# Softmax sums of eight heads per visit to the column-tiled array, in an attention block with program-ordered transfers and a warmed TensorE

## The chip, the cores and the metric

One Trainium2 chip, one core of it. The metric is the device time of one execution in microseconds (us), lower is better. The engines are called PE (TensorE, the matmuls), PEld (its weight loads), DVE (VectorE), ACT (ScalarE), POOL (GpSimd) and SP (SyncE, whose queue issues most transfers).

## The reference

A transformer block with adaptive layer norm: 2048 tokens, width 1024, 32 query heads on 4 key/value heads of 128, the last 512 cached positions, and a SwiGLU feed-forward part (FFN) of width 3584.

```python
mod = (silu(c) @ w_mod).reshape(1, 6, 1, -1)
sa, ca, ga, sb, cb, gb = mod[:, 0], ..., mod[:, 5]
h = layernorm(x) * (1 + ca) + sa
q = h @ wq                                    # 32 heads of 128
p = softmax(q @ k.T * 128 ** -0.5)            # last 512 of 2048 cached positions
x = x + ga * ((p @ v) @ wo)
h = layernorm(x) * (1 + cb) + sb
x = x + gb * ((silu(h @ w_gate) * (h @ w_up)) @ w_down)
```

The inputs and the output are bf16.

## The kernel before

The tokens go in four chunks of 512 (`NTC` = 4), and the attention is a loop over `NU` = 128 steps, one for each head `g` of each chunk. A step computes scores and their exponentials, the projection q of a head three steps ahead, and the output o of the head before. Beside that it does "tasks" that a plan has put at that step. No maximum is subtracted: a bound on the scores (`bound_wq`, `bound_k`, `bound_final`) is computed on the side, and a general path runs if it fails (it does not here).

The softmax denominator of a head is a sum over 512 positions. DVE adds four tiles to one (`psB`), and a matmul with 32 columns of ones sums over the partitions. Four heads make one "visit": their four matmuls sit side by side in a column-tiled array. ACT inverts the sums as exp(-ln), a transfer writes them to DRAM, another reads them back broadcast to all partitions (`rb`, two heads in each), and DVE multiplies the outputs `oT`.

```python
    def emit_l(g):                       # every fourth head
        l_ps = mm("l_ps")
        for i in range(4):
            nc.tensor.matmul(l_ps[32 * i:32 * i + 32, :], lhsT=ones_bf[:, 0:32],
                             rhs=rec.pop(g - 3 + i), start=True, stop=True)
        r = wk.tile([P, TCW], FP32, name="rinv", tag="f32", bufs=2)
        nc.scalar.activation(out=r, in_=l_ps, func=ACT.Ln)
        nc.scalar.activation(out=r, in_=r, func=ACT.Exp, scale=-1.0)
        d = dp.tile([4, TCW], FP32, name="r_d", tag="r_d", bufs=4)
        nc.scalar.dma_start(out=d, in_=r[0:P:32, :])
        rinv[g // 4] = d

    def load_rb(g):                      # two heads later
        ...
        for i in range(2):
            rb = wk.tile([P, 2, TCW], FP32, name="rb", tag="rb", bufs=2)
            nc.sync.dma_start(out=rb, in_=d[2 * i:2 * i + 2, :].partition_broadcast(P))
            rinv[g // 4].append(rb)

    def emit_norm(g):                    # four heads later
        o = oT[(g // H, (g % H) // 4)]
        for i, rb in enumerate(rinv.pop(g // 4)):
            oo = o[:, 2 * i:2 * i + 2, :]
            nc.vector.tensor_tensor(out=oo, in0=oo, in1=rb, op=ALU.mult)
# ... (cut)
    for g in range(3, NU, 4):
        at(g + 2, load_rb, g)
        at(g + 4, emit_norm, g)
    for cc in range(NTC):
        for q in range(NQ):                        # output projection, groups of HQ = 8 heads
            s0 = cc * H + q * HQ + HQ + 4
            for dh in range(DH):
                at(s0 + 4 * dh - 4, load_wo, cc, q, dh)
            for u in range(2 * QT):
                at(s0 + u, emit_wo, cc, q, u)      # one a_ps tile: eight matmuls on oT of 8 heads
        plan_ln((cc + 1) * H + 12, ("h2", cc), cb1, sb)
# ... (cut)
    for k in range(NU + 1):
        if k % 4 == 2 and k + 6 < NU:
            load_wq((k + 6) // H, ((k + 6) % H) // 4)
        if k < NU:
            emit_s(k)
        if k + LEAD < NU:
            emit_q(k + LEAD)
        ...
        run_tasks(k)
        if k >= 1:
            if k % 4 == 0:
                emit_l(k - 1)
            emit_o(k - 1)
```

At the start the first 512 tokens are normalised tile by tile, transposed on PE, and the modulation vectors are made with 128x1 matmuls; then 24 q matmuls of the first three heads run before the loop.

```python
    for t in range(QT):
        ln_stats(t)
        n = ln_norm(t, t % 2 == 0)
        for dt in range(DT):
            nc.tensor.transpose(h0_ps[dt // 4][:, dt % 4, t * P:(t + 1) * P],
                                n[:, dt * P:(dt + 1) * P], ident)
    # ... (cut: modulation columns, then)
        for n in range(4 * LEAD):
            dt, g = (4 * half + n // LEAD, n % LEAD) if half == 0 else (4 + n % 4, n // 4)
            nc.tensor.matmul(q0_ps[g], ...)
```

The kernel leaves the order of instructions on the engines and in the queue of transfers to a scheduler.

Of the kernel before, what the change touches and what calls it, by code (L numbers as in the profile page):

```python
# [9 lines left out]
ALU = mybir.AluOpType  # L10
# [578 lines left out]
def fast_path(ctx, tc, flag, A_x, A_k_cache, A_v_cache, A_wq, A_wo, B_x, B_w_gate, B_w_up,  # L589
# [65 lines left out]
    def load(out, in_, eng=None):  # L655
        with nc.allow_non_contiguous_dma(reason="weight slice"):
            (eng or nc.sync).dma_start(out=out, in_=in_)
# [8 lines left out]
    def load_x(tt):  # L666
        nc.sync.dma_start(out=xt[tt], in_=x2d[tt * P:(tt + 1) * P, :])
# [23 lines left out]
    for kv in range(Hkv):  # L691
        nc.sync.dma_start_transpose(out=kT[:, kv, :], in_=A_k_cache[0, kv, k0:k0 + W, :])
# [11 lines left out]
    nc.vector.memset(eps_t, eps)  # L704
    modT = const.tile([P, 4, DT], FP32, name="modT")
    sa, ca1, sb, cb1 = (modT[:, i, :] for i in range(4))
    ga_bc = const.tile([P, D], FP32, name="ga_bc")
    gb_bc = const.tile([P, D], FP32, name="gb_bc")
# [35 lines left out]
    def load_rows(vecs, part):  # L744
        wm_rows.append([])
        for vec in vecs:
            t = hpool.tile([P, 4, D], BF16, name="wmr", tag="hT")
            load(t, wm_v[:, 4 * part:4 * part + 4, vec * D:(vec + 1) * D])
            wm_rows[-1].append(t)

    def mod_rows(n, part):
        ps = mm("row_ps")
        tiles = wm_rows.pop()
# [9 lines left out]
        else:  # L763
# [3 lines left out]
            nc.sync.dma_start(out=d, in_=r[0:P:32, :])  # L767
            row_d[n] = d

    def load_gate(n, k, dst):  # L770
        nc.sync.dma_start(out=dst.rearrange("p (a b) -> p a b", a=2),
                          in_=row_d[n][k:k + 2, :].partition_broadcast(P))

    def load_cols(n, k, dst, add_one):
        src = row_d[n][k:k + 2, :].rearrange("a (b p) -> p (a b)", p=P)
        with nc.allow_non_contiguous_dma(reason="1024 values to columns"):
            nc.sync.dma_start(out=dst, in_=src)
# [12 lines left out]
    def ln_stats(tt):  # L790
        st = sm.tile([P, DH, nc.vector.BN_STATS_DIM], FP32, name="st", tag="st")
        for i in range(DH):
            nc.vector.bn_stats(out=st[:, i, :], in_=xt[tt][:, i * 512:(i + 1) * 512])  # L793
# [6 lines left out]
    def ln_norm(tt, on_act=False):  # L800
# [7 lines left out]
        else:  # L808
            nc.vector.tensor_scalar(out=n, in0=xt[tt], scalar1=mv[:, 0:1], scalar2=mv[:, 2:3],
                                    op0=ALU.subtract, op1=ALU.mult)  # L810
# [7 lines left out]
    def ln_xpose(key, tt):  # L818
        t = tt % QT
        if t == 0:  # L820
            new_hT(key)
        nc.sync.dma_start_transpose(out=hT[key][:, :, t * P:(t + 1) * P], in_=xn.pop(tt))

    def ln_affine(key, dt, ps, sc, sh, on_act):
# [3 lines left out]
        else:  # L828
            nc.vector.tensor_scalar(out=hT[key][:, dt, :], in0=ps, scalar1=sc[:, dt:dt + 1],
                                    scalar2=sh[:, dt:dt + 1], op0=ALU.mult, op1=ALU.add)  # L830
# [4 lines left out]
    def new_hT(key):  # L835
        hT[key] = hpool.tile([P, DT, TCW], BF16, name="hT", tag="hT")

# [24 lines left out]
# [3 lines that stand above are left out]
        for dt in range(DT):  # L865
            nc.tensor.transpose(h0_ps[dt // 4][:, dt % 4, t * P:(t + 1) * P],
                                n[:, dt * P:(dt + 1) * P], ident)
    q0_ps = []
# [20 lines left out]
    def bound_wq(hg, i, j):  # L889
        w = wq_tiles[(0, hg, i)][:, 2 * j:2 * j + 2, :]  # L890
        junk = wk.tile([P, 2, 512], BF16, name="junk", tag="psA", bufs=2)
        col = (hg * 2 + i) * 2 + j
        nc.vector.scalar_tensor_tensor(out=junk, in0=w, scalar=1.0, in1=w, op0=ALU.mult,  # L893
                                       op1=ALU.mult, accum_out=sq[:, col:col + 1])
# [6 lines left out]
    def bound_k():  # L901
        kk = sm.tile([P, Hkv * WT], FP32, name="kk", tag="kk", bufs=1)
        for i in range(Hkv * WT):
            junk = wk.tile([P, Dh], BF16, name="junk", tag="psA", bufs=2)
            src = k_ld[0][:, i // WT, i % WT, :]
            nc.vector.scalar_tensor_tensor(out=junk, in0=src, scalar=1.0, in1=src, op0=ALU.mult,
                                           op1=ALU.mult, accum_out=kk[:, i:i + 1])
# [8 lines left out]
    def bound_final():  # L916
# [3 lines left out]
        nc.sync.dma_start(out=d, in_=gd)  # L920
        row = wk.tile([1, P, 4], FP32, name="gd_row", tag="f32", bufs=2)
        nc.sync.dma_start(out=row, in_=d)
# [22 lines left out]
    rinv = {}  # L945
    acc = {}
# [12 lines left out]
    def emit_s(g):  # L959
# [14 lines left out]
        b = wk.tile([P, TCW], BF16, name="psB", tag="psB", bufs=5)  # L974
# [3 lines left out]
    def emit_l(g):  # L978


        l_ps = mm("l_ps")
        for i in range(4):
            nc.tensor.matmul(l_ps[32 * i:32 * i + 32, :], lhsT=ones_bf[:, 0:32],  # L983
                             rhs=rec.pop(g - 3 + i), start=True, stop=True)
        r = wk.tile([P, TCW], FP32, name="rinv", tag="f32", bufs=2)
        nc.scalar.activation(out=r, in_=l_ps, func=ACT.Ln)
        nc.scalar.activation(out=r, in_=r, func=ACT.Exp, scale=-1.0)
        d = dp.tile([4, TCW], FP32, name="r_d", tag="r_d", bufs=4)
        nc.scalar.dma_start(out=d, in_=r[0:P:32, :])
        rinv[g // 4] = d  # L990

    def load_rb(g):
        d = rinv[g // 4]
        rinv[g // 4] = []
        for i in range(2):
            rb = wk.tile([P, 2, TCW], FP32, name="rb", tag="rb", bufs=2)
            nc.sync.dma_start(out=rb, in_=d[2 * i:2 * i + 2, :].partition_broadcast(P))
            rinv[g // 4].append(rb)

    def emit_norm(g):  # L1000
        o = oT[(g // H, (g % H) // 4)]
        for i, rb in enumerate(rinv.pop(g // 4)):
            oo = o[:, 2 * i:2 * i + 2, :]
            nc.vector.tensor_tensor(out=oo, in0=oo, in1=rb, op=ALU.mult)  # L1004
# [14 lines left out]
    def load_wo(cc, q, dh):  # L1019
        for i in range(2):  # L1020
            t = blkC("wo", [P, 4, 512])
# [182 lines left out]
```

## Time and profile before

| | before |
|---|---|
| time, median of the first 3 runs | 1295.99 us |
| span of the profiled run | 1293.1 us |
| PE busy | 1274.6 us |
| 5760 matmuls of 512 columns, 216 ns each (estimate of the floor) | about 1244 us |
| first score matmul | 28.15 us |
| first gate/up matmul (end of the attention loop) | 688.29 us |

The page of the profile before: the start of its busy table and the slices of PE and DVE (each digit is the busy share of a fortieth of the span, in tenths):

```profile
span 1293.1 us, 15465 instructions
PE 1274.6 (99%) x6169; PEld 575.1 (44%) x6169; DVE 653.4 (51%) x1144; ACT 454.0 (35%) x646; POOL 0.7 (0%) x6
...
PE   6999999999999999999999999999999999999998
...
DVE  5999768975569655597654641221222211222122
```

PE is the bound everywhere but in the first slice, and DVE is nearly as full at about 30 to 130 us. So a change can gain only what PE does beside the 5760 matmuls, or stop a wait.

The windows of the start, before (bounds and length in us, then busy time and instructions of PE, PEld, DVE, ACT and POOL, the granted clock, the share of transfers, GB/s), cut where the records of the granted clock change:

```profile
19.77:23.18 3.41, 2.90 (x68) 2.17 (x67) 0.98 (x6) 0.70 (x1) 0.00 (x0) 1.00 1.24 176
23.18:26.60 3.42, 3.42 (x10) 1.22 (x9) 1.09 (x2) 0.86 (x2) 0.00 (x0) 0.50 0.93 209
```

PE was at full clock for 3.41 us, then again at half clock for 3.42 us. In the half-clock window only eight 512-column matmuls start (the ten in the view include two that reach into it): one each 427 ns, not each 216. The Trainium skill ("TensorE: Matmul & The Clock Gate", Part 1, What's actually happening) tells of the same: a cold array runs at half clock, and busy-ness is judged in free-running windows of 3413 ns. The 3.41 us and the 427 ns agree.

One visit of the softmax sums, before, in the timeline of PE (start us, busy us, engine, line, operation, count):

```profile
41.56 1.89 PE L953 MATMUL q_ps<-hT,wq 128*128 128x512 bf16 x8
43.38 0.40 PE L983 MATMUL l_ps<-psB,ones_bf 128*32 128x512 bf16 x4
43.71 0.61 PE L1014 MATMUL o_ps<-pT,v_sb 128*128 128x512 bf16 x2
```

The eighth q matmul starts at 41.56 + 7 x 0.216 = 43.07, and the first o matmul at 43.71. Without the visit it would start 0.216 after the q, so the visit costs 0.42 us; by the starts in the trace it is 425 ns (the median; one of the 32 holds a wait as well), 32 times, 13.6 us. The matmuls themselves start 3 ns apart; the price is the way in and out. The Trainium skill ("TensorEngine Tiling (Array Packing)", Key Properties) says that a change of the tiling mode drains the array; it gives no figure, and the trace shows about 93 ns more than the usual 216 on the way in and 106 on the way out.

The waits of PE from 26 us on, before (what waited for what: us in total, times, longest):

```profile
PE a_ps L1031 <- DVE qT L855: 1.2, 1, 1.2
PE l_ps L983 <- DVE psB L975: 0.9, 1, 0.9
PE s_ps L966 <- ACT pT L968: 0.6, 2, 0.3
PE a_ps L1031 <- DVE oT L1004: 0.5, 1, 0.5
```

From the groups of the page before, the normalisation (busy us, mean ns of one, idle of DVE before it), and the start of the line of shares of the chain that ended last:

```profile
L1004 DVE TENSOR_TENSOR oT<-oT,rb 128x1024 bf16<-128x1024 bf16 x64 | 78.0, 1223 | 20.6 <-DMA rb<-r_d 20.5
PE 93%; DVE 4%; DMA 1%; issue 1%; ACT 0%; SPq 0%; DVEq 0%
```

DVE already stood idle for 20.5 us waiting for broadcasts, yet PE waited for a normalised `oT` only 0.5 us: that idle time was slack.

### The profile page before, as it was taken

What the parts mean: (1) busy time and instruction counts of PE and PEld (TensorE: products, weight loads), DVE (VectorE), ACT (ScalarE), POOL (GpSimd) and SP (SyncE); (2) the same over time, 40 slices, a digit from 0 to 9 for tenths busy, and PEclk for the clock granted to TensorE, in tenths of its full rate; (3) what the DMA queues carried; (4) which work ended last, traced back from release to release, by engine and by line L of the source; (5) the groups of instructions that cost most, each with busy time, mean ns of one, the idle gap of its engine ahead of it and who ended that gap; (6) DMA issues with size and microseconds to landing.
All of it is one profiled execution on the core that took longest, in us unless ns stands there. A gap on an engine that the chain in (4) does not pass through costs nothing.

```text
span 1293.1 us, 15465 instructions
## 1 busy us (share of the span) xinstructions
PE 1274.6 (99%) x6169; PEld 575.1 (44%) x6169; DVE 653.4 (51%) x1144; ACT 454.0 (35%) x646; POOL 0.7 (0%) x6
## 2 busy tenths in 40 slices
PE   6999999999999999999999999999999999999998
PEld 3444444444444444444444444444444444444444
DVE  5999768975569655597654641221222211222122
ACT  3755545655455555555453441001100111011100
POOL 0000000000000000000000000000000000000000
PEclk9999999999999999999999999999999999999999
DMA  9897584665354645355447475453536445454402
GB/s 303 273 320 215 206 203 144 187 172 177 122 184 137 180 139 172 130 156 171 163 137 232 161 224 180 145 191 131 165 105 215 167 144 180 137 191 131 147 18 83
DMA packets 219939, 221.08 MB, mean 171 GB/s; under 512 B 45385, under 2 KB 205129, under 8 KB 219858
## 3 DMA queue, kind: packets, MB, share of 16 engines
q1 hardware_dynamic: 214690, 215.54, 52.6%
q10 hardware_dynamic: 5168, 4.46, 1.0%
q8 instruction: 50, 0.82, 0.2%
q14 instruction: 31, 0.25, 0.1%
HBM read 207.63 MB, written 4.47 MB: 164 GB/s over the span
## 4 chain that ended last, share of the span: by engine, by line
PE 93%; DVE 4%; DMA 1%; issue 1%; ACT 0%; SPq 0%; DVEq 0%
PE gu_ps L1099 30%; PE a_ps L1031 17%; PE d_ps L1119 15%; PE q_ps L953 15%; PE o_ps L1014 8%; PE s_ps L966 7%; DVE junk L893 1%; PE l_ps L983 1%; PE q_ps L878 1%; DVE psA L973 1%; DVE qT L855 1%; DMA rb<-r_d 1%; DVE st L793 0%; DMA hT<-xn 0%; DVE psB L975 0%
## 5 line engine op out<-in xcount | busy, mean ns | idle before, releaser
L968 ACT ACTIVATE pT<-s_ps 128x1024 bf16<-128x1024 f32 x256 | 249.0, 1028 | 8.7 <-PE s_ps L966 5.3
L1031 PE MATMUL a_ps<-wo,oT 128*128 128x512 bf16 x1024 | 242.3, 379 | 1.7 <-DVE qT L855 1.2
L953 PE MATMUL q_ps<-hT,wq 128*128 128x512 bf16 x1000 | 237.1, 380 | 0.3 <-DVE modT L730 0.3
L1104 ACT ACTIVATE sg<-gu_ps 128x512 bf16<-128x512 f32 x112 | 66.9, 597 | 460.4 <-PE gu_ps L1099 306.6
L1105 DVE TENSOR_TENSOR guT<-gu_ps,sg 128x512 bf16<-128x512 f32 x112 | 77.5, 692 | 280.8 <-ACT sg L1104 280.8
L1099 PE MATMUL gu_ps<-hT,wu 128*128 128x512 bf16 x896 | 211.8, 379 | 0.0
L1099 PE MATMUL gu_ps<-hT,wg 128*128 128x512 bf16 x896 | 211.7, 379 | 0.0
L1119 PE MATMUL d_ps<-wd,guT 128*128 128x512 bf16 (+2 forms) x952 | 194.2, 367 | 0.0
L1031 PEld LDWEIGHTS <-oT 128*128 128x128 bf16 x1024 | 99.6, 98 | 123.8 <-issue 2.8
L1016 ACT CAST oT<-o_ps 128x512 bf16<-128x512 f32 x128 | 74.3, 580 | 226.3 <-PE o_ps L1014 226.3
L953 PEld LDWEIGHTS <-wq 128*128 128x128 bf16 x1000 | 97.6, 98 | 118.3 <-issue 0.3
L1119 PEld LDWEIGHTS <-guT 128*128 128x128 bf16 x952 | 90.7, 98 | 103.1
L1099 PEld LDWEIGHTS <-wg 128*128 128x128 bf16 x896 | 87.5, 98 | 105.8
L1099 PEld LDWEIGHTS <-wu 128*128 128x128 bf16 x896 | 87.4, 98 | 106.0 <-DMA wu<-in_B_w_up_dram 0.4
L966 PE MATMUL s_ps<-qT,kT 128*128 128x512 bf16 x512 | 131.8, 379 | 0.6 <-ACT pT L968 0.6
L1014 PE MATMUL o_ps<-pT,v_sb 128*128 128x512 bf16 x512 | 131.8, 380 | 0.0
L973 DVE TENSOR_TENSOR psA<-pT 128x1024 bf16<-128x1024 bf16 x128 | 88.2, 689 | 72.5 <-ACT pT L968 72.3
L855 DVE CAST qT<-q_ps 128x512 bf16<-128x512 f32 x128 | 87.8, 688 | 52.9 <-PE q_ps L953 50.7
L1004 DVE TENSOR_TENSOR oT<-oT,rb 128x1024 bf16<-128x1024 bf16 x64 | 78.0, 1223 | 20.6 <-DMA rb<-r_d 20.5
L966 PEld LDWEIGHTS <-kT 128*128 128x128 bf16 x512 | 50.0, 98 | 61.5 <-issue 1.3
L1014 PEld LDWEIGHTS <-v_sb 128*128 128x128 bf16 x512 | 47.3, 98 | 61.7 <-issue 9.0
L975 DVE TENSOR_TENSOR psB<-psA 128x512 bf16<-128x512 bf16 x128 | 53.8, 421 | 0.6
(267 smaller groups left out, 454.2 us busy)
## 6 DMA issues: line engine op xcount, KB each, us to landing
wq<-in_A_wq_dram SPq DMA_DIRECT2D x64, 512.0 KB
rb<-r_d SPq DMA_DIRECT2D x64, 512.0 KB
wo<-in_A_wo_dram SPq DMA_DIRECT2D x64, 512.0 KB
wg<-in_B_w_gate_dram SPq DMA_DIRECT2D x56, 512.0 KB
wu<-in_B_w_up_dram SPq DMA_DIRECT2D x56, 512.0 KB
wd<-in_B_w_down_dram SPq DMA_DIRECT2D x56, 512.0 KB
wmr<-in_w_mod_dram SPq DMA_DIRECT2D x8, 1024.0 KB
out_dram<-o_sb ACTq DMA_DIRECT2D x31, 128.0 KB
```

Of the source, the lines that this page charges most:

```text
L855: nc.vector.tensor_copy(out=t, in_=q_ps)
L953: nc.tensor.matmul(q_ps, lhsT=wq_tiles[(cc, h // 4, dt // 4)][:, dt % 4, (h % 4) * P:(h % 4 + 1) * P], rhs=hT[("h1", cc)][:, dt, :], start ...
L966: nc.tensor.matmul(s_ps[:, i, :], lhsT=kT[:, kv, j * P:(j + 1) * P], rhs=qT[g], start=True, stop=True)
L968: nc.scalar.activation(out=p[:, 2 * jj:2 * jj + 2, :], in_=s_ps, func=ACT.Exp, scale=scale)
L973: nc.vector.tensor_tensor(out=a, in0=p[:, 0:2, :], in1=p[:, 2:4, :], op=ALU.add)
L1004: nc.vector.tensor_tensor(out=oo, in0=oo, in1=rb, op=ALU.mult)
L1014: nc.tensor.matmul(o_ps, lhsT=v_sb[:, kv, j, :], rhs=pT[g][:, j, :], start=(j == 0), stop=(j == WT - 1))
L1016: nc.scalar.copy(out=oT[(cc, hg)][:, hi, :], in_=o_ps)
L1031: nc.tensor.matmul(a_ps, lhsT=oT[(cc, 2 * q + i)][:, hh % 4, t * P:(t + 1) * P], rhs=wo_tiles[(cc, q, dh, i)][:, hh % 4, :], start=(hh == ...
L1099: nc.tensor.matmul(ps[:, n, :], lhsT=gu_w[(cc, fg, nm, dt // 4)][:, dt % 4, fi * P:(fi + 1) * P], rhs=hT[("h2", cc)][:, dt, :], start=(dt ...
L1105: nc.vector.tensor_tensor(out=guT[(cc, fg)][:, fi, :], in0=ps[:, 1, :], in1=g, op=ALU.mult)
L1119: nc.tensor.matmul(d_ps, lhsT=guT[(cc, f // 4)][:, f % 4, t * P:(t + 1) * P], rhs=wd_tiles[(cc, dh, f // 4)][:, f % 4, c0:c0 + w], start=( ...
```

## The change

Its intent: fewer visits to the column-tiled array (16 of eight heads in place of 32 of four); PE kept busy with constant matmuls at the start so that its clock is up earlier; the transfers and the larger DVE steps held in program order (`pin` in the code, "pinned" below), and the bound's DVE work spread over later chunks; one buffer for both output gates; the last chunk's layer norm with its reciprocal root on DVE. Cut to its core:

```diff
+    stage = {"dma": True, "steps": False}
+    def pin(ins, what="steps"):
+        return tc.keep_in_program_order(ins) if stage[what] else ins
+    def fetch(out, in_):
+        pin(nc.sync.dma_start(out=out, in_=in_), "dma")      # used for nearly all transfers
# ... (cut)
+    def warm(n):
+        for _ in range(n):
+            tc.keep_in_program_order(
+                nc.tensor.matmul(warm_ps, lhsT=ones_bf, rhs=warm_w, start=True, stop=True))
+    warm(16)
# ... (cut: in the loop over the first four tiles, after the transposes of each)
+        warm(2)
# ... (cut: bound_wq reads the weights of chunks 1 to 3 in place of chunk 0;
#      bound_k and bound_final move to the last chunk; big DVE steps get pin())
-            b = wk.tile([P, TCW], BF16, name="psB", tag="psB", bufs=5)
+            b = wk.tile([P, TCW], BF16, name="psB", tag="psB", bufs=9)
     def emit_l(g):
-        l_ps = mm("l_ps")
-        for i in range(4):
-            ...
+        d = dp.tile([HQ, TCW], FP32, name="r_d", tag="r_d", bufs=2)
+        l_ps = [mm("l_ps") for _ in range(2)]
+        for i in range(HQ):
+            a = 32 * (i % 4)
+            nc.tensor.matmul(l_ps[i // 4][a:a + 32, :], lhsT=ones_bf[:, 0:32],
+                             rhs=rec.pop(g - HQ + 1 + i), start=True, stop=True)
+        for n in range(2):
+            r = wk.tile([P, TCW], FP32, name="rinv", tag="f32", bufs=2)
+            ... Ln, Exp, transfer to d ...
+    def load_rb(g, n):
+        rb = wk.tile([P, 2, TCW], FP32, name="rb", tag="rb", bufs=2)
+        fetch(out=rb, in_=rinv[g // HQ][2 * n:2 * n + 2, :].partition_broadcast(P))
+        rbs.append(rb)
# ... (cut)
-    for g in range(3, NU, 4):
-        at(g + 2, load_rb, g)
-        at(g + 4, emit_norm, g)
+    for g in range(HQ - 1, NU, HQ):
+        for n in range(4):
+            at(g + 2 + n // 2 * 2, load_rb, g, n)
+            at(g + 4 + n // 2, emit_norm, g, n)
-            s0 = cc * H + q * HQ + HQ + 4
+            s0 = cc * H + q * HQ + HQ + 5
-        plan_ln((cc + 1) * H + 12, ("h2", cc), cb1, sb)
+        plan = plan_ln if cc < NTC - 1 else plan_late_ln
+        plan((cc + 1) * H + 13, ("h2", cc), cb1, sb)
# ... (cut)
+    at(15, load_gate, 0, 0, ga_bc)
+    at(NU + 14, gate_b)                    # the FFN gate goes into the attention gate's buffer
+    stage["steps"] = True
     for k in range(NU + 1):
-            if k % 4 == 0:
+            if k % HQ == 0:
                 emit_l(k - 1)
+    stage.update(dma=False, steps=False)   # before the FFN's loop
```

## The prediction

> **What bounds the kernel.** TensorE. Busy table: PE 1274.6 of 1293.1 us, DVE 51%, ACT 35%, DMA about half. By the starts of matmuls in the trace, 512-column matmuls follow every 216 ns nearly everywhere. There are 5760 of them in q, s, o, a, gate/up and down; 5760 x 0.216 is about 1243 us, a floor that the change leaves (an estimate from that cadence). Only about 50 us are to be had:
> - 0 to 28.15 us, until the first score matmul: 24 q matmuls (5.2 us of work) plus 23 us of start. Most of these q matmuls come every 427 ns. The clock records show full clock from 19.8, half again from 23.2 to 26.6, then full. This agrees with the Trainium skill, "TensorE: Matmul & The Clock Gate", Part 1 (a cold array runs at half clock; busy-ness is judged in free-running windows of 3413 ns).
> - 32 visits to the column-tiled array for softmax sums (l). From the last matmul to the first l 309 ns; four l's 3 ns apart; then 322. Less the 216 owed anyway, 424 ns a visit, 13.6 us. The skill's "TensorEngine Tiling (Array Packing)", Key Properties, says a mode switch drains the array; the excess (93 ns in, 106 out) agrees.
> - 4 visits for modulation rows, about 1.06 us each: kept.
> - PE waits after 28 us (PE timeline): 0.9 on ACT's first exponentials, 0.67 at 77 us and 1.39 at 180 us on a busy DVE.
> - About 5 us after the last matmul: kept.
>
> **What the change does.**
> 1. Eight heads per visit: 16 visits. The second four share the columns of the first; in row visits such a group follows after about 207 ns. A visit: 309+9+207+9+322-216 = 640 ns, 10.2 us in all. Gain 3.3 us, all on the critical path. Two l buffers at once squeeze the four small PSUM buffers; I expect little waiting.
> 2. Constant matmuls: 16 at the start, two after each transposed tile. PE did nothing until 7.37 us; the 16 take about 7, and delay the first transpose little. Warm, the 24 q matmuls would save up to 4 us, but the first twelve are fed by hT evictions 0.69 us apart (17.4 us for the last), and DMA delivers the second half of the modulation weights only at about 18 to 19 us. So 2 to 3 us if warm. PE stays half idle there, so the clock may drop again: I count 2 us.
> 3. Program order for transfers and DVE steps; the bound's 1.2 us DVE pieces leave the first 32 heads (DVE 100% busy at 50 to 100 us) for later ones (70%). Of 2.1 us of DVE-caused waits I count 1.5 gone. The 0.9 on ACT stays.
> 4. Gate buffer, last LN's rstd on DVE (most ACT table loads of 1.28 us near 730 to 753 us go): off the path; PE lost 0.06 us there.
>
> **Sum.** 3.3 + 2 + 1.5 = 6.8 us off 1295: **1288 us**, range 1283 to 1293. Faster by over 2%: 1%; same 98%; slower 1%.
>
> **What shows it.** l: 16 visits at 640 ns. Clock records: full before 15 us, q at 216 ns at 15 to 26 us; first score matmul at about 25.5 to 26.5. PE waits on DVE between 70 and 190 us under 0.5 us. Gate/up and down unchanged at 216 ns.
>
> **What would make it wrong.** The clock drops back during the half-idle start (step 2 then gains nothing; the dummy matmuls cost up to 1 us); pinned transfers block one another; in-order DVE steps delay q evictions; new PSUM waits after l.

## The result, and the profile after

| | before | after |
|---|---|---|
| median | 1294.53 us (4 runs, 1292.82 to 1296.79) | 1298.10 us (4 runs, 1296.42 to 1299.53) |
| ratio | | 1.0026 (95%: 1.0003 to 1.0049) |
| profiled span | 1293.1 us | 1294.6 us |

A ratio here and below is from runs of both kernels in the same rounds, so not quite the ratio of the medians or means given. A second measurement of the changed kernel beside eleven runs of before (experiment e5) gave 1.0019 (1.0000 to 1.0038). The class predicted, "within 2%", holds. But 1288 us with a range of 1283 to 1293 was predicted, and the kernel took 1296 to 1299: the seven microseconds of gain are not there, and by the means the kernel is 1.5 (e5) to 3.4 us slower. Both profiles of it are of the fastest of its executions in their set, so their waits are rather below the usual.

The page after, the same lines:

```profile
span 1294.6 us, 15331 instructions
PE 1268.8 (98%) x6074; PEld 575.2 (44%) x6193; DVE 653.0 (50%) x1159; ACT 431.1 (33%) x625; POOL 1.2 (0%) x7
...
PE   7999999999999999999999999999999999999998
...
DVE  5476668976698867587864651221222211222122
```

PEld counts 6193 loads and PE only 6074 matmuls: some matmul records are missing, so PE's busy time is not to be compared. DVE's load at 30 to 130 us has become even, as the change meant.

The windows of the start, after (columns as before):

```profile
7.55:10.96 3.41, 1.91 (x22) 1.24 (x22) 3.41 (x15) 1.23 (x4) 0.00 (x0) 1.00 1.08 364
10.96:14.38 3.42, 2.24 (x73) 2.06 (x71) 1.16 (x6) 2.08 (x5) 0.00 (x0) 1.00 1.10 348
14.38:17.79 3.41, 3.19 (x17) 1.80 (x16) 0.93 (x2) 1.24 (x2) 0.00 (x0) 0.50 1.11 350
```

The constant matmuls bring full clock at 4.14 us, far sooner than before. But at 14.38 the clock drops for 3.41 us, after a window in which PE was busy for 2.24 of 3.42 us, and the drop falls on transposes and the first q matmuls. The window before that had PE busy for less, 1.91 us, and the clock stayed up. The two differ in kind as well: the first held transposes and constant matmuls of 512 columns, the second 63 matmuls of 128x1.

One visit, after, in the timeline of PE:

```profile
55.60 1.89 PE L1024 MATMUL q_ps<-hT,wq 128*128 128x512 bf16 x8
57.42 0.61 PE L1056 MATMUL l_ps<-psB,ones_bf 128*32 128x512 bf16 x8
57.96 1.04 PE L1083 MATMUL o_ps<-pT,v_sb 128*128 128x512 bf16 x3
```

The last q starts at 57.11, the first o at 57.96: 0.85 us, 0.63 above 0.216. By the starts it is 640 or 641 ns in fifteen of the sixteen visits (805 in the other), 10.4 us in all, as predicted. The parts were each about 10 ns off and cancel: the second four follow after 216 ns, not 207, and the way out is 312, not 322.

The waits of PE from 26 us on, after:

```profile
PE a_ps L1099 <- DVE oT L1073: 4.3, 6, 1.6
PE s_ps L1037 <- ACT pT L1039: 1.5, 3, 0.9
PE gu_ps L1175 <- DMA wu<-in_B_w_up_dram: 1.4, 1, 1.4
PE gu_ps L1175 <- DVE guT L1181: 0.5, 1, 0.5
```

The 1.2 us and 0.9 us behind a busy DVE are gone. In their place the output projection (`a_ps`) waits six times, 4.3 us, for a normalised `oT`, and the FFN waits 1.4 us for an up-weight.

From the groups of the page after, and the shares of the chain that ended last, by engine:

```profile
L1073 DVE TENSOR_TENSOR oT<-oT,rb 128x1024 bf16<-128x1024 bf16 x64 | 76.8, 1221 | 19.5 <-DMA rb<-r_d 19.4
PE 87%; DVE 5%; DMA 4%; ACT 1%; SPq 1%; issue 1%; DVEq 0%
```

DVE's idle time on broadcasts is about the same as before, 19.4 us. But its longest single wait is now 2.8 us and not 1.7, and the chain has moved: DMA 4% in place of 1%, PE 87% in place of 93%. Here is one such place, from the chain that ended last, after, at 240 us (start us, length us, what):

```profile
240.69 0.08 DVE junk L958
240.77 2.28 DVE oT L1073 x2
243.06 0.02 issue
243.07 6.77 DMA rb<-r_d
249.84 0.02 issue
249.87 1.24 DVE oT L1073
251.10 0.05 issue
251.15 0.60 PE a_ps L1099 x2
```

The first two normalisations end at 241.91 and 243.04, and each frees one of the two `rb` buffers. Only then can the next broadcast go (issued at 241.94 and 243.07); the last of the four lands 6.77 us after its issue, its normalisation starts at 249.87, and PE, which needs all eight heads in an `a_ps` tile, waits 1.61 us for it.

Where the profiled runs gained and lost, by the first score matmul and the first gate/up matmul:

| stage | before | after | difference |
|---|---|---|---|
| start, to the first score matmul | 28.15 | 27.00 | -1.15 |
| attention loop, to the first gate/up matmul | 660.14 | 658.93 | -1.21 |
| the rest | 604.8 | 608.7 | +3.9 |

One `a_ps` tile, eight matmuls or 1.73 us, moved from the second stage to the third, because the projection starts one head later. With it put back, the attention loop is 0.5 us longer in spite of 3.3 us saved in visits, and the rest is 2.2 us longer.

### The profile page after: what moved, and what is told of

It is laid out like the page before. It is cut to its first block, busy times and chain, and to the rows that moved or that the text cites. A ratio compares the mean times of both kernels' runs of the same rounds, so it can differ in the third digit from the quotient of the medians. Undisturbed runs are those within 1.5% of the kernel's fastest.

```text
span 1294.6 us, 15331 instructions
## 1 busy us (share of the span) xinstructions
PE 1268.8 (98%) x6074; PEld 575.2 (44%) x6193; DVE 653.0 (50%) x1159; ACT 431.1 (33%) x625; POOL 1.2 (0%) x7
## 4 chain that ended last, share of the span: by engine, by line
PE 87%; DVE 5%; DMA 4%; ACT 1%; SPq 1%; issue 1%; DVEq 0%
PE gu_ps L1175 29%; PE d_ps L1195 15%; PE a_ps L1099 15%; PE q_ps L1024 14%; PE o_ps L1083 7%; PE s_ps L1037 7%; DMA rb<-r_d 2%; DVE oT L1073 2%; DMA wm_1_119<-in_w_mod_dram 1%; ACT pT L1039 1%; SPq L664 1%; PE l_ps L1056 1%; DVE psA L1044 1%; DVE junk L958 0%; DMA modT<-row_d 0%
## 5 line engine op out<-in xcount | busy, mean ns | idle before, releaser
L1039 ACT ACTIVATE pT<-s_ps 128x1024 bf16<-128x1024 f32 x256 | 251.6, 1029 | 26.0 <-PE s_ps L1037 26.0
L1024 PE MATMUL q_ps<-hT,wq 128*128 128x512 bf16 x972 | 233.5, 379 | 1.0 <-DVE modT L752 0.3
L1073 DVE TENSOR_TENSOR oT<-oT,rb 128x1024 bf16<-128x1024 bf16 x64 | 76.8, 1221 | 19.5 <-DMA rb<-r_d 19.4
```

The costliest lines, as they stand in the source:

```text
L1024: nc.tensor.matmul(q_ps, lhsT=wq_tiles[(cc, h // 4, dt // 4)][:, dt % 4, (h % 4) * P:(h % 4 + 1) * P], rhs=hT[("h1", cc)][:, dt, :], start ...
L1039: nc.scalar.activation(out=p[:, 2 * jj:2 * jj + 2, :], in_=s_ps, func=ACT.Exp, scale=scale)
L1073: pin(nc.vector.tensor_tensor(out=oo, in0=oo, in1=rbs.pop(0), op=ALU.mult))
```

## The experiments

Seventeen kernels were run, in five groups; each group shares its runs of before. All results were correct.

The first theory was that the eight-head visit makes the normalisations late (and that more slack, or fewer of them at once, brings the gain back). Its rivals were that the last layer norm on DVE and the FFN's transfers cost the time, and that the constant matmuls cost what they gain.

### e1: the output projection two heads later

```diff
-    at(NU + 14, gate_b)
+    at(NU + 17, gate_b)
-            s0 = cc * H + q * HQ + HQ + 5
+            s0 = cc * H + q * HQ + HQ + 7
```

> The changed kernel with the output projection of each eight heads started two heads later (7 instead of 5 heads after the eight are complete) and the second gate loaded three steps later, nothing else. In the trace of the changed kernel PE waited 4.3 us in six places for a normalised oT, whose broadcast sums (second pair of the eight heads) landed too late. Theory A (the eight-head visit brings all normalisations of a projection group into one burst with two broadcast buffers, and the burst is late): these waits fall from 4.3 us to under 0.5, and the time falls by 3.5 to 4.5 us against the changed kernel. Rival B (in-order transfers and DVE steps cost PE time wherever they stand): the wait only moves, PE's waits after 26 us stay at 6 to 8 us in all, the time stays within 1.5 us.

Measured: median 1295.23 us, ratio 0.9996 (0.9982 to 1.0010), 6 runs. The wait of `a_ps` for `oT` is gone. But other waits came: 1.8 us of scores on ACT, 1.3 us of q and 1.0 us of l on DVE's accumulation, 0.8 on an up-weight, 0.7 on `hT`. So slack removes the wait that was named and recovers part of the loss (about 3 us by the ratios, which are from different rounds), but not the predicted gain: the work is still bunched, and other waits take the place of the one removed.

### e2: the last layer norm as it was

```diff
-        plan = plan_ln if cc < NTC - 1 else plan_late_ln
+        plan = plan_ln
```

> The changed kernel with the last layer norm as before (Ln and Exp on ACT, one tile each two steps). Theory A: in the changed kernel the last layer norm's rows became ready together, three transposes stood in one row in the transfer queue (6.0 us of issue) ahead of an up-weight load, and PE waited 1.4+0.5 us near 765 us. With the old norm the transposes are spread again and these 2 us of waiting go; time 1.5 to 2.2 us less than the changed kernel, although the ACT table loads (1.28 us each) return. Rival: the table loads hold up the gate activations and PE waits just as long: no change in time.

Measured: median 1297.14 us, ratio 1.0012 (0.9998 to 1.0026), 6 runs. Gate/up matmuls at 709 to 767 us still wait, 0.9 us on `guT` and 0.7 on up-weights, and `a_ps` still waits 3.5 us for `oT`. The theory that the layer norm is what costs in the FFN found no support; if the layer norm costs anything, this run can't resolve it.

### e3: the change without constant matmuls; e4: before with constant matmuls only

```diff
 # e3, from the changed kernel
-    warm_ps = mm("warm_ps")
-    warm(16)
+    warm(0)
-        warm(2)
+        warm(0)
 # e4, from the kernel before
+    warm_ps = mm("warm_ps")
+    warm(16)
+        warm(2)
```

> The changed kernel without its constant matmuls (no 16 at the start, no two after each tile). Theory W (they help a little): the first score matmul, at 27.0 us in the changed kernel, moves back to about 28, and the time rises by about 1 us. Rival C (the dummies leave the array colder later in some executions: the three other runs of the changed kernel show a granted clock of 0.996 to 0.997 and spans 1.6 to 3.2 us longer than the profiled one's at 0.999): without them the clock is 0.999 in all runs and the time falls by 1 to 2 us.

> The kernel before with the constant matmuls alone added. Theory W: first score matmul at 26 to 27.3 us instead of 28.15, time 1 to 2 us less than before. Rival C: some executions show a granted clock of 0.996 to 0.997 and the mean time is equal to or above before's.

Measured: e3 median 1297.58 us, ratio 1.0006 (0.9987 to 1.0024); e4 median 1297.67 us, ratio 1.0009 (0.9992 to 1.0026); 6 runs each. Neither shows a gain from constant matmuls. In e4's profile the first score matmul came at 25.84 us, 2.3 sooner than before, so in that run the start was won as predicted; in e3 it came at 26.67 without any constant matmul, against 27.00 and 27.60 in two profiles of the changed kernel.

The clock records of all nineteen profiles show where the gain goes. In all ten kernels with constant matmuls the clock dropped to half between 12.9 and 14.7 us, for 3.4 or 6.8 us (in e10 once more at 23.7). Of the nine without, three (e3, e12, e15) got full clock at 17.1 to 18.4 us and kept it; six (before, e8, e13, e14, e16, e17) got it at 18.8 to 20.4 us and lost it again after one window of 3.41 us, for another. The first score matmul came at 26.6 to 26.7 us in the three, at 27.7 to 28.5 in the six, and at 25.8 to 28.1 with constant matmuls. By the means (27.7 without, 26.8 with) constant matmuls win 0.9 us of the start, not 2, and in some kernels part of that is lost just after, to waits of q for its next weights at 30 to 32 us (1.0 us in e2, 0.6 in e6, 0.9 in e11; but 0.4 in e15 too, without them). Why the clock falls is not shown. Busy time as the profile counts it does not decide: a window with 1.91 us kept the full clock (the changed kernel), one with 2.90 us lost it (before). At the start every window behind which it fell held 32 to 63 of the 128x1 matmuls, and gaps; but a window of e4 with 64 of them and PE busy for 3.16 us kept it. No run tells the two apart.

e4's profile shows a second thing, in the middle of the program. Two windows of it at 178 to 185 us (columns as before):

```profile
178.54:181.96 3.42, 1.27 (x7) 0.52 (x6) 3.42 (x8) 1.05 (x2) 0.00 (x0) 1.00 0.95 257
181.96:185.37 3.41, 3.41 (x9) 1.18 (x8) 3.41 (x7) 0.00 (x0) 0.00 (x0) 0.50 0.43 134
```

A single wait of PE for DVE, 2.3 us long, left PE busy for 1.27 of 3.42 us; the next window ran at half clock, eight matmuls started in place of about sixteen, and that cost 1.7 us more. Here a wait cost PE nearly twice its length.

### e5: the changed kernel again; e6: the change with four heads per visit

```diff
 # e6, from the changed kernel: emit_l, load_rb and emit_norm of before, pinned
-            if k % HQ == 0:
+            if k % 4 == 0:
                 emit_l(k - 1)
-    for g in range(HQ - 1, NU, HQ):
-        for n in range(4):
-            at(g + 2 + n // 2 * 2, load_rb, g, n)
-            at(g + 4 + n // 2, emit_norm, g, n)
+    for g in range(3, NU, 4):
+        for n in range(2):
+            at(g + 2, load_rb, g, n)
+            at(g + 4, emit_norm, g, n)
```

> The changed kernel once more, beside the others of this call. On record so far: 1298.0 mean of 4 against 1294.7 of before's 4, but before's runs in the second set had a mean of 1296.3. If the loss is real, it is 1 to 3 us over before here too; in the trace PE waits on normalised oT 3.5 to 4.7 us and 1 to 2.5 us near 760 to 767 us (gate/up weights or guT), as in the runs that kept both parts.

> The changed kernel with softmax sums of four heads per visit, as before (32 visits), all else of the change kept. Theory A (eight heads per visit put the normalisations of a group into one late burst): waits on oT fall from about 4 us to under 1; the visits cost 13.6 instead of 10.2 us; sum: 0 to 1.5 us less than the changed kernel. Rival B (pinned order makes the waits): the oT waits stay at 3 us or more and the time rises by about 3 us.

Measured: e5 median 1297.20 us, ratio 1.0019 (1.0000 to 1.0038); e6 median 1292.51 us, ratio 0.9980 (0.9961 to 0.9999); 5 runs each, on one chip and in the same rounds. By the means (1297.05 and 1292.59), eight heads per visit cost 4.5 us against four, where 3.3 us of gain were predicted; no run of e6 is as slow as the fastest of e5. The groups of the page of e6, the normalisation:

```profile
L1071 DVE TENSOR_TENSOR oT<-oT,rb 128x1024 bf16<-128x1024 bf16 x64 | 75.4, 1219 | 1.6 <-DMA rb<-r_d 1.6
```

With four heads DVE waits 1.6 us for broadcasts, not 19.4, and PE not at all for `oT`. The rest of the change is a gain of about 3 us with four heads per visit.

### e7: projection two heads later and the last layer norm eleven later; e8: before with eight heads only

```diff
 # e7, from the changed kernel
-            s0 = cc * H + q * HQ + HQ + 5
+            s0 = cc * H + q * HQ + HQ + 7
-        plan((cc + 1) * H + 13, ("h2", cc), cb1, sb)
+        plan((cc + 1) * H + (13 if cc < NTC - 1 else 24), ("h2", cc), cb1, sb)
-    at(NU + 14, gate_b)
+    at(NU + 22, gate_b)
 # e8: the eight-head emit_l, load_rb, emit_norm, psB of nine buffers, s0 + 5 and the
 # single gate buffer of the change, put into the kernel before, without pins
```

> The changed kernel with the output projection two heads later (as in the run that moved it alone) and the last layer norm 11 and the second gate's load 8 steps later, so that transposes, gate and down-weights no longer meet the up-weight load near 760 us. If that meeting makes the wait there (and not the arithmetic of the last norm): no PE wait over 0.3 us between 740 and 775 us, time 1 to 2 us less than the run with the projection alone moved (mean 1295.4 beside a before of 1296.3), so 2 to 3 us less than before. If not, waits of 1 us or more stay near 700 to 770 us.

> The kernel before with eight heads per visit (and the single gate buffer, which its memory needs), no program order, no dummies, bound and last norm as before. Theory A: 16 visits of about 640 ns (3.3 us saved), but 3 us or more of new PE waits on normalised oT; the time within 1.5 us of before's. Rival B (pins make the waits): no such waits, 3 us less than before.

Measured: e7 median 1295.14 us, ratio 1.0000 (0.9983 to 1.0017); e8 median 1294.55 us, ratio 0.9995 (0.9978 to 1.0013); 6 runs each. e7 is no better than e1: more room for the layer norm buys nothing that these runs resolve. e8 gets under 1 us of the 3.3 us, with 2.2 us of `a_ps` waiting for `oT` and 2.7 us of o waiting for q's eviction in its profile. So the eight-head visit falls short in the old order of instructions too; the pins are not needed for that.

### e9: four heads, with no pins inside the loop

```diff
 # from e6
-    stage["steps"] = True
+    stage["dma"] = False
```

> The run with four heads per visit (mean 1292.6, 0.998 of before), now without program order for transfers and without it for DVE steps; the moved bound, dummies and last norm stay. Theory P (program order is what made that run steady: five runs within 1.0 us, no PE wait on DVE between 33 and 700 us): without it waits of 0.5 to 2 us on DVE come back between 70 and 190 us and the time rises by 1 to 3 us. Rival M (moving the bound's DVE work out of the first 32 heads is what did it): no such waits, time within 0.7 us of 1292.6.

Measured: median 1305.41 us, ratio 1.0079 (1.0065 to 1.0094), 5 runs; 12.7 us slower than e6 by the means, which are from different groups and chips (the kernel before had 1295.62 and 1295.53 there). DVE's idle time on broadcasts, in the view of waits, e9:

```profile
DVE oT L1071 <- DMA rb<-r_d: 50.0, 25, 3.7
```

The scheduler's order, with the rest of the change in place, is far worse than the program's order. That isn't the same as pins being worth 12.7 us over the kernel before: before had no pins, and its plan left the order to the scheduler, without the changed steps that e9 keeps.

### e10, e11, e12: four heads, and the FFN's order

```diff
 # e10, from e6: two gate buffers, psB of five, the second gate loaded at step 31,
 # the last layer norm as before, and
-            s0 = cc * H + q * HQ + HQ + 5
+            s0 = cc * H + q * HQ + HQ + 4
 # e11: e10 with the projection one head later again
-            s0 = cc * H + q * HQ + HQ + 4
+            s0 = cc * H + q * HQ + HQ + 5
 # e12: e10 without the constant matmuls
-    warm(16)
+    warm(0)
-        warm(2)
+        warm(0)
```

> Four heads per visit, program order, moved bound and dummies kept; two gate buffers, the output projection one head earlier (as before) and the last norm on ACT as before, so that the transfer queue near 700 to 770 us is in the order of the kernel before. Theory: the 1.5 us that PE waited there for an up-weight in the run with four heads goes; no PE wait over 0.3 us after 690 us; time 1 to 1.8 us under that run's 1292.6, about 0.9965 to 0.997 of before. Rival: the wait stays at 1 us or more, the order of the queue is not its cause.

> As the run with the old order near 700 to 770 us, but the output projection one head later, as in the changed kernel: the one difference. If this shift alone (its last weights give their buffers to the down-weights one step later, closer to the up-weight load) makes the wait: 0.8 to 1.6 us of PE waiting near 760 us and 1 to 1.5 us more time. If the gate load or the last norm's transposes made it: no wait, same time within 0.5 us.

> The run with the old order near 700 to 770 us without the constant matmuls. So far the changed kernel without them was no slower than with them, and the kernel before with them no faster than without. Expected: first score matmul 0.3 to 1.5 us later, but up to 1 us of that won back from the wait on the next query weights near 30 to 32 us; time 0 to 1 us more. If dummies gave the 2 us I had counted, it is 2 us more.

Measured, 5 runs each on one chip: e10 median 1291.59 us, ratio 0.9965 (0.9951 to 0.9979); e11 median 1292.67, ratio 0.9976 (0.9962 to 0.9989); e12 median 1291.52, ratio 0.9968 (0.9955 to 0.9982). So with four heads, pinned order, the moved bound and the requests for weights spread over more steps, which came with them, gain 4.3 us by e12's mean (1291.28 against 1295.62). Constant matmuls add nothing (e10 against e12). The projection one head later costs 1.2 us by the means (e11 against e10), but the two intervals overlap, so that is likely, not shown.

The waits of PE from 26 us on in e12 are a single line:

```profile
PE s_ps L1037 <- ACT pT L1039: 0.6, 2, 0.3
```

### e13, e14, e15: reciprocal sums in bf16

The question left was what in the eight-head visit costs: too few `rb` buffers, the bytes of the broadcasts, or the DVE time of the normalisations, all bunched by eight. In these kernels the reciprocal sums are rounded to bf16 before they go to DRAM, so that a broadcast of two heads is 256 KB in place of 512. Results differ slightly from those with f32. All have the old last layer norm, one gate buffer and no constant matmuls, and six buffers in place of five for the tiles tagged `row` (q, the gate's activations and the output among them).

```diff
 # all three, from the changed kernel (e15: with four heads)
-        d = dp.tile([HQ, TCW], FP32, name="r_d", tag="r_d", bufs=2)
+        d = dp.tile([HQ, TCW], BF16, name="r_d", tag="r_d", bufs=2)
-            nc.scalar.activation(out=r, in_=r, func=ACT.Exp, scale=-1.0)
-            nc.scalar.dma_start(out=d[4 * n:4 * n + 4, :], in_=r[0:P:32, :])
+            rh = wk.tile([P, TCW], BF16, name="rinvh", tag="row", bufs=6)
+            nc.scalar.activation(out=rh, in_=r, func=ACT.Exp, scale=-1.0)
+            nc.scalar.dma_start(out=d[4 * n:4 * n + 4, :], in_=rh[0:P:32, :])
-        rb = wk.tile([P, 2, TCW], FP32, name="rb", tag="rb", bufs=2)
+        rb = wk.tile([P, 2, TCW], BF16, name="rb", tag="rb", bufs=2)
 # e13 only: four buffers, all four broadcasts at once
+        rb = wk.tile([P, 2, TCW], BF16, name="rb", tag="rb", bufs=4)
-            at(g + 2 + n // 2 * 2, load_rb, g, n)
+            at(g + 2, load_rb, g, n)
```

> The changed kernel with the old last norm and without dummies (as two earlier runs, each neutral), the reciprocal sums in bf16 and four broadcast buffers instead of two, all four loads issued two heads after the visit (values differ slightly, bf16 reciprocals). If the wait for buffers is the cause: DVE's idle time on the broadcast falls from 17 to 20 us to under 5, PE's waits on oT from about 4 us to under 0.5, and the time is 2 to 3 us under the two-buffer run and at most that of the four-head run. If the burst itself is: DVE still shows PE waits of 3 us or more on qT, acc or oT, time within 1.5 us of the two-buffer run.

> The same with two broadcast buffers and the loads timed as in the changed kernel: the control for bf16 alone. The broadcast has half the bytes, so it lands sooner; I expect DVE's idle time on it at 5 to 15 us and PE waits on oT at 1 to 3 us, time 1 to 3 us under the changed kernel's (about 1.002 of before).

> The same with four heads per visit and two bf16 broadcast buffers: the control for eight against four. PE waits on DVE between 33 and 690 us under 0.3 us, as with f32 sums; time about 0.9975 of before (as the four-head run with the projection one head later).

Measured, 6 runs each on one chip: e13 median 1290.13 us, ratio 0.9955 (0.9938 to 0.9971); e14 median 1289.88, ratio 0.9949 (0.9933 to 0.9965); e15 median 1292.66, ratio 0.9972 (0.9957 to 0.9988). With bf16, four buffers are no better than two. That doesn't clear the buffers with f32, where each broadcast waits for one (see 240 us above): four f32 buffers were not run. And now eight heads gain 2.9 us on four (means 1289.72 and 1292.67), close to the 3.3 us of the visits. No run of e14 is as slow as the fastest of e15. Four heads gain nothing from bf16 and the sixth `row` buffer (0.9972 against 0.9976 and 0.9968 of e11 and e12), so these are no gain by themselves; they take away what the eight-head visit cost. The waits of PE from 26 us on in e14, with none on `oT`; the normalisation in e14's groups; and the same place at 240 us in e14's timeline:

```profile
PE gu_ps L1173 <- DMA wu<-in_B_w_up_dram: 1.7, 1, 1.7
PE s_ps L1034 <- ACT pT L1036: 0.6, 2, 0.3
```

```profile
L1071 DVE TENSOR_TENSOR oT<-oT,rb 128x1024 bf16<-128x1024 bf16 x64 | 41.6, 685 | 4.3 <-DMA rb<-r_d 4.2
```

```profile
241.05 1.29 DVE L1071 TENSOR_TENSOR oT<-oT,rb 128x1024 bf16<-128x1024 bf16 x2
241.77 0.94 SPq L664 DMA_DIRECT2D rb<-r_d  x2
246.87 1.29 DVE L1071 TENSOR_TENSOR oT<-oT,rb 128x1024 bf16<-128x1024 bf16 x2
```

One normalisation takes 0.685 us in place of 1.22, and the second pair is done at 248.16 and not at 251.10. The Trainium skill ("VectorE: DVE Perf Modes", What auto-detection actually checks) says that the mode with two results per cycle is taken if every tensor is of 16 bits; with `rb` in f32 one tensor is not. The measured 1.78 to 1 goes that way, somewhat short of 2 to 1.

### e16: bf16 sums, but the normalisation as slow as with f32

bf16 halves the bytes and shortens the DVE step at once. To part the two, e16 is e14 with the multiplication made by a slower instruction for the same result.

```diff
-        pin(nc.vector.tensor_tensor(out=oo, in0=oo, in1=rbs.pop(0), op=ALU.mult))
+        pin(nc.vector.scalar_tensor_tensor(out=oo, in0=oo, scalar=1.0, in1=rbs.pop(0),
+                                           op0=ALU.mult, op1=ALU.mult))
```

> The run with eight heads, two buffers and bf16 sums, but with the normalisation done by a DVE instruction that takes about 1.2 us for 128x1024 bf16 (the scalar-tensor-tensor form that the bound uses) instead of 0.68. If the bytes of the broadcast made the loss: DVE's idle time on the broadcast stays under 6 us, PE's waits on oT under 0.5 us, the mean within 0.8 us of the bf16 run (1289.7, 0.9949 of before). If the DVE time made it: PE waits of 3 us or more come back and the time goes up to 1.000 to 1.002 of before.

Measured: median 1292.68 us, ratio 0.9970 (0.9956 to 0.9983), 5 runs. The groups of e16, the normalisation, and the waits of PE that e14 didn't have:

```profile
L1071 DVE SCALAR_TENSOR_TENSOR oT<-oT,rb 128x1024 bf16<-128x1024 bf16 x64 | 76.1, 1219 | 4.9 <-DMA rb<-r_d 4.7
```

```profile
PE a_ps L1098 <- DVE oT L1071: 0.8, 2, 0.5
PE o_ps L1082 <- DVE qT L916: 0.8, 1, 0.8
```

1.219 us, as with f32, so DVE's time is restored while the bytes stay halved, and DVE's idle time on broadcasts stays at 4.7 us. Against e14 (0.9949, another chip) it loses 2.9 us by the means, with the pair's end moved from 248.16 to 250.92 us; against e17 below, in the same rounds, 2.5 us. Against eight heads with f32 (e2, 1.0012, in another group, which differs by the constant matmuls and the `row` buffers as well) it gains about 5 us. Neither of the two outcomes expected came: it fell between. So the DVE time of four normalisations in a row counts for 2.5 to 2.9 us; the rest, about 5, goes to the broadcasts of half the bytes if the sixth `row` buffer does nothing with eight heads, as it did with four. Eight heads with f32 sums and six `row` buffers were not run.

### e17: e13 with the projection and normalisations one head earlier

```diff
-            at(g + 4 + n // 2, emit_norm, g, n)
+            at(g + 4, emit_norm, g, n)
-            s0 = cc * H + q * HQ + HQ + 5
+            s0 = cc * H + q * HQ + HQ + 4
```

> Eight heads, bf16 sums in four buffers, all normalisations four heads after the visit, output projection one head earlier as in the kernel before, old last norm, no dummies. Expected: the wait of 1 to 1.9 us for an up-weight near 760 us falls under 0.9 us, visits at 640 ns, no PE wait on oT over 0.5 us in all; 0.993 to 0.995 of before, 1287.5 to 1289.5 us. If the earlier projection meets the normalisations, PE waits on oT come back at 0.3 us or more a group (16 groups) and it is slower than the run with the later projection.

Measured: median 1290.28 us, ratio 0.9950 (0.9936 to 0.9963), 5 runs. It is no better than e14. Its FFN waits 1.4 us on `guT`; taking back the one-head shift did not remove every wait there, so the shift is not the whole cause of them. e14 and e17 are the fastest versions found, both about 6.5 us under before.

### A second reading of all runs: the clock

Each run lists its span and its mean granted clock. Half-clock time costs PE half its length (the Trainium skill, "TensorE: Matmul & The Clock Gate", HAM oscillation — how this bites in real kernels, counts it so), so span x (1 - mean clock) is an estimate of what was lost to it. Over its 51 runs, the kernel before took 1291.4 us (span) where the mean clock was 1.000 (8 runs) and 1296.6 where it was 0.997 (6 runs). The estimate for that step of 0.003 is 3.9 us, and the measured step is 5.1: much of the spread of before's times goes with such windows.

The estimate is rough. The mean is given to three decimals; it counts the half clock after the last matmul, which cost nothing (0 to 2.9 us in the profiles, 2.8 in e15's, so up to 1.4 us in the column below); and it leaves out the cold time ahead of the first record, so a cold start stays in the "rest".

| kernel, runs | heads, sums | constant matmuls | mean span | lost to half clock | rest |
|---|---|---|---|---|---|
| before, 51 | 4, f32 | no | 1294.2 | 2.1 | 1292.1 |
| e4, 6 | 4, f32 | yes | 1295.7 | 3.7 | 1292.0 |
| changed (with e5), 9 | 8, f32 | yes | 1295.7 | 3.9 | 1291.8 |
| e3, 6 | 8, f32 | no | 1295.2 | 0.9 | 1294.4 |
| e6, 5 | 4, f32 | yes | 1290.8 | 2.8 | 1288.0 |
| e10, 5 | 4, f32 | yes | 1289.6 | 2.8 | 1286.7 |
| e12, 5 | 4, f32 | no | 1289.5 | 1.6 | 1288.0 |
| e15, 6 | 4, bf16 | no | 1290.9 | 1.9 | 1288.9 |
| e14, 6 | 8, bf16 | no | 1287.9 | 2.4 | 1285.5 |
| e16, 5 | 8, bf16, slow DVE | no | 1290.8 | 2.1 | 1288.8 |

Three pairs differ in constant matmuls alone (e4 and before, changed and e3, e10 and e12). In each, the kernel with them lost more to half clock, by 1.6, 3.0 and 1.2 us, and in the last two its rest was shorter by about as much (2.6 and 1.3). That fits the drop taking back what was won in the cold start; differences of the size of 1.2 us are within the estimate's error, so it is not shown. Eight heads against four cost 3.8 us in the rest with f32 (changed and e6), and gain 3.4 us with bf16 (e14 and e15), so the clock is not what turns the sign.

## Why the prediction was wrong

**What held.** PE bounds the kernel, and the class is "within 2%". A visit of eight heads costs 641 ns (640 predicted, with some luck: two parts were off by 10 ns in opposite directions). The waits on a busy DVE of 0.9 to 1.2 us in the attention loop went, at the places where they had been. The wait of scores on ACT stayed, as predicted, and grew from 0.6 to 1.5 us in the first profile. Full clock came before 15 us, as predicted, but the first score matmul came at 27.00 us, where 25.5 to 26.5 was predicted.

**The step that failed most, step 1: "Gain 3.3 us, all on the critical path" and "I expect little waiting".** The 3.3 us were read rightly from the visits, and e14 against e15 delivers 2.9 of them. What was left out is that the visit also sets when its results come: eight heads at once mean four broadcasts of 512 KB and four normalisations of 1.22 us in the few heads before the projection, which needs all eight. The prediction looked for the squeeze in the PSUM buffers of the visit (PSUM holds the `_ps` tiles); it was in the transfers and on DVE behind it. Measured: eight heads against four cost 4.5 us (e6 and e5), where -3.3 was predicted. The runs with bf16 show that the DVE time is a part (e16 and e14) and that the f32 broadcasts are the larger one (e16 and e2, with the `row` buffers as a difference left over). Whether more f32 buffers would have helped is open: a broadcast waits for a free buffer, and e13 tried four only with bf16. The 20.5 us of DVE idle on broadcasts in the profile before pointed to the place, but did not measure its slack: with four heads in program order they are 1.6 us (e6).

**Step 2: "I count 2 us".** In time it was none that the runs resolve (e10 and e12, e3 and the changed kernel, e4 and before). The prediction named the cause as a risk, "the clock may drop again", and it is what came: in all ten profiles with constant matmuls the clock fell back at 12.9 to 14.7 us, in a stretch where PE waited for transfers and ran 128x1 matmuls. The 0.9 us by which the first score matmul came sooner was in some kernels lost again to waits for weights.

**Step 3: 1.5 us for program order.** This was too small. Program order with the moved bound and the spread requests for weights, four heads and the old FFN order gains 4.3 us (e12). These were not separated over the kernel before.

**Step 4: "off the path".** The table of stages shows the rest after the attention loop 2.2 us longer, with 1.9 us of waits at gate/up tiles (763 and 767 us) that before didn't have. e11 against e10 puts some 1.2 us on the projection's later start, within overlapping intervals; e2 shows no part of the layer norm; e17 keeps a wait there with the shift undone. In the queue of SP in the changed kernel, the up-weight that PE waited for was issued at 762.32 us behind three transposes that take 5.96 us; before, the like was issued at 760.21. That is an argued cause, not a shown one.

**The sum.** Predicted: -3.3 - 2 - 1.5 + 0 = -6.8 us. Measured parts, by means of the same rounds: order and bound -4.3 (e12), constant matmuls +0.1 (e10), one head later +1.2 (e11), the last layer norm and the gate buffer +0.1 by the means and +0.5 by the ratios (e6 and e11, from two groups, not resolved), eight heads +4.5 (e5 and e6). That is +1.6 to +2.0 us; the changed kernel was measured at +1.5 (e5) and +3.4 (first comparison). The sum closes within the noise. The waits that the view names can be checked against the 4.5 us. The view counts idle time from the modelled end of a matmul; from start to start, less the usual 216 ns, PE's waits inside the attention loop come to 5.7 us in e5's profile (2.9 of them `a_ps` on `oT`), 7.3 in the first profile of the changed kernel (5.3 on `oT`) and 1.7 in e6's. e5's profiled execution is 2.2 us longer than e6's although its visits save 3.3, so 5.5 us are to be found. The loop's waits are 4.0 of them, and the later first score matmul (27.60 against 26.44 us) is 1.2. So in these two profiles waits in the loop make most of the cost. e5's other executions are on average 2.9 us longer than the profiled one and have no profile; what they add is open. Half clock may be a part (1.1 us more than in e6 by the estimate).

## What to carry to other kernels

When a step is batched to save its fixed cost, also price what its results trigger: here a batch twice as large delivered them in bursts twice as large, and the consumer of the last one waited for the burst, not for the average. Where the burst was made of broadcasts and of a DVE step on f32, a bf16 operand paid for the batching twice, in bytes (as far as shown) and in DVE time, although it gained nothing without it. Keeping TensorE busy with constants brought the full clock early, but it gained no time here: the clock fell back in the stretch of gaps and 128x1 matmuls behind them.

## What the Trainium skill lacked or had wrong

- "TensorEngine Tiling (Array Packing)", Key Properties, says that a mode switch drains the array but gives no figure. Here a visit of four 32-column matmuls cost PE 425 ns beyond the usual cadence, one of eight 641 ns; the way in is 93 ns and the way out about 106 ns over the usual 216.
- "TensorE: Matmul & The Clock Gate", Part 1, warns of idle gaps longer than about 3.4 us. Here half clock followed a single wait of 2.3 us (PE busy for 1.27 of a 3.42 us window, e4), a window with PE busy for 2.24 of 3.42 us (after) and even one with 2.90 of 3.41 us, mostly 128x1 matmuls (before). A window with 1.91 of 3.41 us kept it (after, transposes and constant matmuls). The page doesn't say what share of a window keeps the clock, nor how 128x1 matmuls count.
- The same page says that the number of cold matmuls changes from run to run. It does not say how far that spreads the times of one kernel: here they spread over 3 to 7 us within a group, going with the mean granted clock (spans of 1291.4 us at 1.000, 1296.6 at 0.997).
- "VectorE: DVE Perf Modes" has no row for `scalar_tensor_tensor` in its tier table. Here, 128x1024 bf16 took 1.219 us, as long as `tensor_tensor` with one f32 operand (1.22), while `tensor_tensor` in bf16 took 0.685.
- No page read gives the time of a broadcast from DRAM to all partitions with other transfers behind it. Here a 512 KB broadcast landed 6.77 us after its buffer came free (after, at 243.07 us); DVE stood idle for the last 1.20 us of that.
